# Splitting the W1 load into pieces of 3, 2, 3 and 4 column blocks, with the x tiles moved behind them

## The chip, the cores and the metric

The kernel runs on one core of one Trainium2 chip. The metric is the device time of one execution in microseconds (us), as a median over repeated executions. Kernels are compared only within the same rounds. The span of a profile is about 1.7 us shorter than the device time of the same run.

## The reference

A transformer block with two branches in parallel on the same normalised input. The change touches only the layer norm and the first matrix product of the second branch.

```python
xn = _layernorm(x)                        # x: 2048 x 640, bf16
return x + _A_ref(xn, wqkv, wo) + _B_ref(xn, w1, b1, w2, b2)

def _B_ref(x, w1, b1, w2, b2):            # w1: 640 x 1536
    h = _gelu(jnp.einsum("bsd,df->bsf", x, w1) + b1)
    return jnp.einsum("bsf,fd->bsd", h, w2) + b2
# _A_ref: linear attention with 32 heads; not touched by the change
```

## The kernel before

The 2048 tokens are 16 tiles of 128. A tile is loaded (`dma_x`), VectorE takes its statistics in two halves (`ln_half`) and aggregates them (`ln_aggr`), GpSimd makes rstd (one over the standard deviation), and VectorE normalises (`ln_norm`). The normalised tile must then be transposed. Tiles 0 to 2 are transposed by TensorE, and the result is copied out of PSUM, the memory that TensorE writes to. Tiles 3 to 15 are transposed by a DMA. Below, x3 is the load of tile 3, xn(2) the normalised tile 2 and xnT(2) its transpose, and so on. `W1` has 12 column blocks of 128 (`JT` = 12), loaded in four pieces. A unit `(t0, n, jb)` of the first matrix product (the first GEMM below) multiplies block `jb` with `n` tiles from tile `t0` on: five matmuls of n x 128 columns, then a Gelu on ScalarE. `plan` is the order in which TensorE (PE in the profile) runs the units. "T1" and "T2" in it are the places of the transposes of tiles 1 and 2.

```python
W1P = [(i * F // 4, (i + 1) * F // 4) for i in range(4)]      # four pieces of 3 blocks
...
dma_x(0, 1); dma_x(1, 1)                                      # one queue, in this order
dma_w1(0); dma_w1(1)
dma_x(2, 1); dma_x(3, 1)
dma_w1(2); dma_x(4, 2); dma_w1(3); dma_x(6, 2)
...
def copy2(t, b0, b1):      # xnT(t) out of PSUM: 3 parts by ScalarE, 2 by VectorE  (cut)
def h_unit(t0, n, jb):     # reads the W1 piece of jb and xnT of its tiles          (cut)
...
plan = h_list(0, 1, 0, 3) + ["T1"] + h_list(0, 1, 3, 6) + h_list(1, 1, 0, 6)
plan += h_list(0, 2, 6, 7) + ["T2"] + h_list(0, 2, 7, 9) + h_list(2, 1, 0, 9) + h_list(0, 3, 9, JT)
plan += h_list(3, 1, 0, 3) + h_list(4, 1, 0, 3) + h_list(3, 2, 3, JT) + h_list(5, 3, 0, JT)
plan += h_list(8, 2, 0, 3) + h_list(10, 2, 0, 3) + h_list(8, 4, 3, JT) + h_list(12, 4, 0, JT)
for u in plan:
    if u == "T1":
        transp2(1, b, b + 1); copy2(1, b, b + 1)
        ln_stats(2); ln_half(3, 0); ln_half(3, 1); ln_norm(2); ln_aggr(3); ln_half(4, 0)
    elif u == "T2":
        b = transp(2); xnT_copy(2, b)
        ln_norm(3); xnT_dma(3); ln_half(4, 1); ln_aggr(4); ln_rest()
    else:
        h_unit(*u)
```

Each engine runs its instructions in the order in which they stand. So an instruction that waits for a late tile holds up whatever stands behind it on its engine, even work on another tile.

## Time and profile before

| kernel before | |
|---|---|
| device time, 3 runs | 207.26 us median (207.16 to 207.52) |
| profiled run: time, span | 207.4 us, 205.6 us |
| PE busy | 202.2 us, 98% of the span |
| first GEMM: its first matmul, its end (where the chain passes to the next stage) | 6.63 us, 59.75 us |
| T2 transposes begin | 10.99 us |

From the page of the kernel before: its engines' busy time, and the engines of the chain of waits that ended last.

```profile
PE 202.2 (98%) x1539; PEld 135.2 (66%) x1539; DVE 109.6 (53%) x227; ACT 71.4 (35%) x133; POOL 35.1 (17%) x85
...
PE 96%; DVE 1%; DMA 1%; issue 0%; ACT 0%; DVEq 0%
```

PE is nearly always busy and the chain runs through it, so a change elsewhere shows only where it makes PE wait or stop waiting. The chain in order of time shows where that could be. Its columns are start, length and what; L380 is the first GEMM, L318 and L361 are the transposes T1 and T2, L488 is the stage behind the first GEMM.

```profile
6.63 1.00 PE ps L380 x15
7.63 0.28 PE ps L318 x5
7.91 0.01 issue
7.92 3.23 PE ps L380 x50
11.15 0.28 PE ps L361 x5
11.43 48.32 PE ps L380 x340
59.75 21.73 PE ps L488 x160
```

No visible gap. But the ends of matmuls are modelled in this view, and short waits hide in their tails. The weight loads (PEld) show them better. From their timeline (start, busy time, engine, line, operation, count, then in brackets the idle time before it and what ended it):

```profile
6.60 0.85 PEld L380 LDWEIGHTS ps<-xnT,W 128*128 128x128 bf16 x15 [0.23 <-DMA W<-in_B_w_dram]
7.41 0.32 PEld L318 LDWEIGHTS ps<-ident,xn_tm 128*128 128x128 bf16 x5
7.92 2.95 PEld L380 LDWEIGHTS ps<-xnT,W 128*128 128x128 bf16 x50 [0.19 <-DMA W<-in_B_w_dram]
10.88 0.37 PEld L361 LDWEIGHTS ps<-ident,xn_tm 128*128 128x128 bf16 x5
```

The third line is the one hole that the change can close: PE stands 0.19 us for the second W1 piece. The fourth line has no bracket: the transposes of tile 2 come when PE gets to them, and xn(2) is already there. How much earlier is read on VectorE (DVE):

```profile
7.95 0.29 DVE L327 COPY xnT<-ps 128x256 bf16<-128x256 bf16 x1 [0.80 <-PE ps L318]
8.36 0.89 DVE L331 BATCH_NORM_STATS2 stats<-xPK 128x6 f32<-128x320 bf16 x2
9.35 0.21 DVE L339 BATCH_NORM_AGGREGATE aggr<-stats 128x2 f32<-128x12 f32 x1
9.47 0.83 DVE L331 BATCH_NORM_STATS2 stats<-xPK 128x6 f32<-128x320 bf16 x2
10.32 0.45 DVE L353 TENSOR_SCALAR xn_tm<-xPK,aggr,rstd 128x640 bf16<-128x640 bf16 x1
```

These are, in order, the copy for tile 1, the statistics of tile 2, both halves of tile 3's statistics, and the normalisation of tile 2. It ends at 10.77 us (10.32 + 0.45), 0.11 us before PE's weight loads for it begin (10.88).

### The profile page before, as it was taken

The page shows a single profiled execution, that of the slowest core. Times are in us where ns is not written, and L with a number is a line of the kernel's source. Part 1 is how long each engine was busy: PE and PEld are TensorE (multiplying, and loading weights), DVE is VectorE, ACT ScalarE, POOL GpSimd, SP SyncE. Part 2 cuts the span into 40 slices and gives each one's busy share as a digit, 9 for nine tenths or more (in the row PEclk, how much of TensorE's full clock was granted, in tenths as well). Part 3 has the DMA queues.
Part 4 walks back from the last instruction along what each step waited for, and adds up shares of the span by engine and source line. Part 5 has one row for each costly group of instructions (what it writes and reads, how often), then busy time and mean ns, then how long its engine had stood idle before and what let it go on. Part 6 is the DMA issues. An engine that isn't in the chain of part 4 may idle for free.

```text
span 205.6 us, 3863 instructions
## 1 busy us (share of the span) xinstructions
PE 202.2 (98%) x1539; PEld 135.2 (66%) x1539; DVE 109.6 (53%) x227; ACT 71.4 (35%) x133; POOL 35.1 (17%) x85
## 2 busy tenths in 40 slices
PE   8999999999999999999999999999999999999995
PEld 3898767544457777777746445677777777777774
DVE  3784388100007888999358888734764322523322
ACT  2787777666676455111153554300000000000000
POOL 3342156800000001999000200000000000000000
PEclk9999999999999999999999999999999999999999
DMA  5967846699920000000000000968611100100111
GB/s 153 351 169 122 204 127 123 81 360 327 368 90 0 0 0 3 0 0 3 0 0 3 2 0 19 364 182 171 152 64 63 35 32 32 37 32 32 35 37 59
DMA packets 24842, 19.69 MB, mean 96 GB/s; under 512 B 9976, under 2 KB 24824, under 8 KB 24824
## 3 DMA queue, kind: packets, MB, share of 16 engines
q1 hardware_dynamic: 23072, 17.86, 29.5%
q10 hardware_dynamic: 1752, 1.58, 4.1%
q8 instruction: 12, 0.20, 0.4%
q14 instruction: 6, 0.05, 0.1%
HBM read 13.11 MB, written 2.62 MB: 77 GB/s over the span
## 4 chain that ended last, share of the span: by engine, by line
PE 96%; DVE 1%; DMA 1%; issue 0%; ACT 0%; DVEq 0%
PE ps L671 36%; PE ps L380 26%; PE ps L513 11%; PE ps L488 11%; PE ps L554 10%; DMA xPK<-in_A_x_dram 1%; DVE stats L331 1%; PE ps L608 1%; PE ps L564 1%; PE ps L618 1%; PE ps L318 0%; DVE xn_tm L353 0%; DVE W L722 0%; PE ps L361 0%; PE ps L537 0%
## 5 line engine op out<-in xcount | busy, mean ns | idle before, releaser
L671 PE MATMUL ps<-W,HG 128*128 128x320 bf16 (+2 forms) x396 | 54.8, 295 | 0.0
L380 PE MATMUL ps<-xnT,W 128*128 128x128 bf16 (+3 forms) x405 | 52.7, 292 | 0.1
L671 PEld LDWEIGHTS ps<-W,HG 128*128 128x128 bf16 x396 | 38.1, 98 | 14.5 <-ACT Msb L590 0.2
L380 PEld LDWEIGHTS ps<-xnT,W 128*128 128x128 bf16 x405 | 33.8, 98 | 18.4 <-DMA W<-in_B_w_dram 0.4
L384 ACT ACTIVATE HG<-ps,b1c 128x128 bf16<-128x128 f32 (+3 forms) x81 | 39.1, 515 | 14.4 <-PE ps L380 13.3
L682 DVE TENSOR_TENSOR W<-ps,xnT 128x640 bf16<-128x640 f32 x15 | 12.4, 825 | 35.8 <-PE ps L671 34.6
L476 ACT ACTIVATE ek<-ps 128x512 bf16<-128x512 f32 (+1 forms) x36 | 23.2, 645 | 20.4 <-PE ps L554 10.7
L477 DVE TENSOR_SCALAR ek<-ek 128x512 bf16<-128x512 bf16 (+1 forms) x36 | 11.0, 305 | 32.4 <-ACT ek L476 31.2
L671 PE MATMUL ps<-Msb,PQ 128*128 128x320 bf16 (+2 forms) x165 | 24.2, 295 | 0.0
L554 PE MATMUL ps<-xnT,Wqkv 128*128 128x512 bf16 x100 | 21.9, 379 | 0.0
L513 PE MATMUL ps<-xPK,xn_tm 128*128 128x320 bf16 x160 | 21.9, 299 | 0.0
L488 PE MATMUL ps<-Wqkv,xnT 128*128 128x320 bf16 x160 | 21.9, 299 | 0.0
L671 PEld LDWEIGHTS ps<-Msb,PQ 128*128 128x128 bf16 x165 | 15.9, 98 | 5.9
L488 PEld LDWEIGHTS ps<-Wqkv,xnT 128*128 128x128 bf16 x160 | 15.7, 98 | 6.2
L513 PEld LDWEIGHTS ps<-xPK,xn_tm 128*128 128x128 bf16 x160 | 15.7, 98 | 6.1
L507 POOL COPY Wqkv<-Wqkv 128x128 bf16<-128x128 bf16 x25 | 15.1, 603 | 22.9 <-PE ps L488 21.4
L331 DVE BATCH_NORM_STATS2 stats<-xPK 128x6 f32<-128x320 bf16 x32 | 14.0, 477 | 9.3 <-DMA xPK<-in_A_x_dram 9.2
L554 PEld LDWEIGHTS ps<-xnT,Wqkv 128*128 128x128 bf16 x100 | 9.7, 98 | 11.4
L479 DVE SCALAR_TENSOR_TENSOR PQ<-ps,ek 128x512 bf16<-128x512 f32 x20 | 13.8, 692 | 2.1
L479 DVE SCALAR_TENSOR_TENSOR xPK<-ps,ek 128x640 bf16<-128x640 f32 x16 | 13.2, 825 | 1.7
L525 DVE TENSOR_TENSOR Msb<-Msb,xPK 128x640 f32<-128x640 f32 x14 | 11.6, 825 | 0.5
L341 POOL TENSOR_TENSOR rstd<-aggr,mhalf 128x1 f32<-128x1 f32 x16 | 9.9, 620 | 8.9 <-DVE aggr L339 8.9
(57 smaller groups left out, 77.4 us busy)
## 6 DMA issues: line engine op xcount, KB each, us to landing
xnT<-in_A_x_dram SPq DMA_DIRECT2D x4, 640.0 KB, 6.8
Wqkv<-in_A_wqkv_dram SPq DMA_DIRECT2D x3, 800.0 KB, 6.8
out_dram<-W SPq DMA_DIRECT2D x15, 160.0 KB, 1.8
W<-in_B_w_dram SPq DMA_DIRECT2D x4, 480.0 KB, 6.1
W<-in_B_w_dram SPq DMA_DIRECT2D x1, 1920.0 KB, 13.0
xn_tm<-rden ACTq DMA_DIRECT2D x12, 128.0 KB, 3.4
xPK<-in_A_x_dram SPq DMA_DIRECT2D x4, 320.0 KB, 5.5
Wo<-in_A_wo_dram SPq DMA_DIRECT2D x8, 160.0 KB, 8.4
```

The lines of the kernel that those rows point to most:

```text
L331: Pl.ins(v, lambda e: e.bn_stats(stats[:, s, 6 * h:6 * h + 6], x_in[:, t, h * HW:(h + 1) * HW]), reads=r_x[t], writes=[r_stats[s][h]])
L380: Pl.ins(pe, [(lambda e, k=k: e.matmul(bank(b, 0, w), W1[:, k, jb * P:(jb + 1) * P], xnT[:, k, tok], start=(k == 0), stop=(k == DT - 1))) ...
L384: Pl.ins(s_, lambda e: e.activation(HG[:, jb, tok], bank(b, 0, w), ACT.Gelu_apprx_tanh, bias=b1c[:, jb:jb + 1]), reads=[B_[b], r_b1c], wri ...
L476: Pl.ins(s_, lambda e: e.activation(e2, src, ACT.Exp), reads=br, writes=[r_ek[s]])
L479: Pl.ins(v, lambda e: e.scalar_tensor_tensor(out=d2, in0=src, scalar=0.0, in1=e2, op0=ALU.max, op1=ALU.add), reads=br + [r_ek[s]], writes= ...
L488: fns.append(lambda e, k=k, h=h, b=b, t=t: e.matmul(bank(b + h, 0, HW), xnT[:, k, t * P:(t + 1) * P], Wqkv[:, k, D + h * HW:D + (h + 1) * ...
L507: Pl.ins(g, lambda e, k=k, i=i: e.tensor_copy(plain(Wqkv[:, k, D:2 * D], i), parts(Wqkv[:, k, 0:D], i)), reads=[r_Wq], writes=[r_Wk, r_WqP])
L513: Pl.ins(pe, [(lambda e, t=t, h=h, b=b, f=f, i=i: e.matmul(bank(b + h, 0, HW), xn_tm[:, t, f * P:(f + 1) * P], PK[:, t, h * HW:(h + 1) * H ...
L525: Pl.ins(v, lambda e, t=t: e.tensor_tensor(out=zsum, in0=zsum, in1=PK[:, t, :], op=ALU.add), reads=[r_PK[t], r_zsum], writes=[r_zsum])
L554: Pl.ins(pe, [(lambda e, k=k, j=j, b=b: e.matmul(bank(b), Wqkv[:, k, D + j * P:D + (j + 1) * P], xnT[:, k, cc], start=(k == 0), stop=(k == ...
L671: Pl.ins(pe, [(lambda e, i=i, x=x, bb=bb: e.matmul(bank(bb, 0, x[1] - x[0]), seq[i][0], seq[i][1][:, x[0]:x[1]], start=(i == 0), stop=(i = ...
L682: Pl.ins(v, lambda e: e.tensor_tensor(out=halves(out_sb[:, s, :]), in0=pair(b), in1=halves(x_res[:, t, :]), op=ALU.add), reads=B_[b:b + 2] ...
```

## The change

The intent is to let the loads follow what TensorE needs first. The second W1 piece becomes smaller, so that it lands sooner. x3 moves behind the third piece, x4 and x5 behind the fourth, where x6 and x7 already stood. The plan follows the new pieces, which saves two units (81 to 79, ten matmuls), and VectorE's order is adapted to x3 and x4 coming later.

```diff
-        W1P = [(i * F // 4, (i + 1) * F // 4) for i in range(4)]
+        W1J = [0, JT // 4, JT * 5 // 12, JT * 8 // 12, JT]
+        W1P = [(lo * P, hi * P) for lo, hi in zip(W1J, W1J[1:])]
@@
         dma_w1(0)
         dma_w1(1)
         dma_x(2, 1)
+        dma_w1(2)
         dma_x(3, 1)
-        dma_w1(2)
+        dma_w1(3)
         dma_x(4, 2)
-        dma_w1(3)
         dma_x(6, 2)
@@
-        plan = h_list(0, 1, 0, 3) + ["T1"] + h_list(0, 1, 3, 6) + h_list(1, 1, 0, 6)
-        plan += h_list(0, 2, 6, 7) + ["T2"] + h_list(0, 2, 7, 9) + h_list(2, 1, 0, 9) + h_list(0, 3, 9, JT)
+        j1, j2, j3 = W1J[1:4]                                  # 3, 5, 8
+        plan = h_list(0, 1, 0, j1) + ["T1"] + h_list(0, 1, j1, j2) + h_list(1, 1, 0, j2)
+        plan += h_list(0, 2, j2, j2 + 1) + ["T2"] + h_list(0, 2, j2 + 1, j3) + h_list(2, 1, 0, j3) + h_list(0, 3, j3, JT)
@@ at T1
                 ln_stats(2)
                 ln_half(3, 0)
+                ln_norm(2)
                 ln_half(3, 1)
-                ln_norm(2)
                 ln_aggr(3)
-                ln_half(4, 0)
@@ at T2
-                ln_half(4, 1)
-                ln_aggr(4)
+                ln_stats(4)
                 ln_rest()
```

## The prediction

> **What bounds the kernel now.** The page gives PE 202.2 of the 205.6 us span (98%), and the chain of waits is 96% PE; from 6.63 us to the end it is an unbroken row of matmuls. The change can win only (a) a hole in PE before 12 us, or (b) matmul time, and can lose only by opening a hole.
>
> (a) In the view of waits, the first GEMM's weight loads idle 0.4 us behind W1 DMAs, in two pieces. The first is at the start, untouched. The second lies before 7.92 us: tile 1's transposes are through at about 7.74, and the second W1 piece lands at 7.9 (issued 2.2, 5.7 us to landing). Worth 0.18 us.
>
> (b) The plan shrinks from 81 to 79 units (405 to 395 matmuls) with equal columns. In the timeline, 45 matmuls of 128 columns and 5 of 256 between 7.92 and 10.99 make about 56 ns for 128 columns, where the Trainium skill ("TensorE: Matmul & The Clock Gate", "Wait — 56ns, not 53.3ns?") has N/2.4 GHz plus about 2.5 ns; the trace agrees. Ten fewer are worth 0.03 us. So at most 0.2 us of 207 can be won.
>
> **What moves.** In 6 to 12 us the queue runs at 316 to 372 GB/s (windows), about the 358 GB/s HBM limit per core of the skill's "DMA: Bandwidth & Descriptors", "Specifications"; so order alone matters, and landings follow cumulative bytes. Measured landings: W1 first 6.4, second 7.9, x2 8.36, x3 8.7, third 10.3, x4-5 11.2, fourth 12.65, x6-7 13.4. Estimates for the new order: second 7.45, x2 7.9, third 9.4, x3 9.8, fourth 11.7, x4-5 12.5, x6-7 13.4. x3 comes a microsecond later.
>
> **The new start (estimates).**
> 1. Tile 1's transposes end 7.74; piece two is there: 0.18 us gained.
> 2. Only two units (10 matmuls, 0.56 us) now stand before tile 1's own units, which need ScalarE's copy of xnT(1); that ended at 8.41 and doesn't move. PE waits from 8.30 to about 8.47: the gain goes back.
> 3. 25 matmuls of 128 and 5 of 256 columns: PE reaches T2 at about 10.4; piece three is there.
> 4. T2 transposes xn(2). VectorE's tile 1 copy lasts to 8.24, so stats(2) starts only 0.1 earlier (8.26), rstd(2) is ready about 10.1. In front of norm(2) stands the first half of stats(3), now waiting for x3: 9.8 to 10.25. Norm(2) ends about 10.7; the transposes begin 10.65 to 10.85. Before, T2 came after 7 blocks on two tiles (10.99 us), which hid this chain; now after 6. PE waits 0.25 to 0.45 us.
> 5. Then PE has 10 x 107, 40 x 56 and 20 x 160 ns to tile 3's first unit: about 17.5 against 17.28 before. Tiles 4 to 7 are normalised some 0.5 us later, but tile 4's transpose lands near 17.7, needed at 18.4; later margins are about 1 us. No further hole.
>
> **Prediction.** +0.25 us: 207.5 us, 207.05 to 207.95 in 8 of 10. Faster by over 2%: 1%; within 2%: 98%; slower by over 2%: 1%.
>
> **What would show it.** No weight-load wait on a W1 DMA near 7.9; new PE waits on ScalarE's xnT copy near 8.3, and of 0.2 to 0.45 us at T2 on VectorE's xn_tm; stats(3) waiting for x3; 395 matmuls on the first GEMM's line; PE unbroken from 12 us on.
>
> **What would make it wrong.** x3 landing near 9.4 [...] leaves T2 waiting only 0.2 us: about 207.3. After 10.2 costs more. If tile 4 or the fourth piece came a microsecond late, a hole would open after 15 us.

## The result

The changed kernel took 207.80 us in the median (207.54 to 208.00, 6 runs) against 207.33 us for the kernel before (207.16 to 207.52, 6 runs). The ratio is 1.0021, with a 95% interval of 1.0008 to 1.0034. The change is thus about 0.44 us slower: within 2%, but clear of the noise.

| profiled run | before | after |
|---|---|---|
| device time, us | 207.40 | 207.81 |
| PE busy, us | 202.2 | 202.9 |
| matmuls of the first GEMM | 405 | 395 |
| first matmul of the first GEMM, us | 6.63 | 6.92 |
| T2 transposes begin, us | 10.99 | 10.90 |
| from there to the end of the first GEMM, us | 48.76 | 49.30 |
| end of the first GEMM, us | 59.75 | 60.20 |

From the page of the changed kernel:

```profile
PE 202.9 (98%) x1529; PEld 135.4 (66%) x1529; DVE 109.6 (53%) x227; ACT 71.1 (34%) x131; POOL 35.1 (17%) x85
...
PE 98%; DVE 0%; issue 0%
```

PE has ten matmuls fewer and yet 0.7 us more busy time. Some 0.5 us of that are filler matmuls that ran longer at the start (below); and the waits of this section hide in modelled tails, so that the page counts them as busy. This is why a busy share of 98% proves nothing here. The chain of the changed kernel in order of time (L381 is the first GEMM, L319 and L362 are the transposes T1 and T2):

```profile
6.97 0.95 PE ps L381 x15
7.92 0.28 PE ps L319 x5
8.20 0.56 PE ps L381 x10
8.76 0.00 issue
8.76 2.11 PE ps L381 x30
10.87 0.02 issue
10.90 0.45 PE ps L362 x5
11.35 48.85 PE ps L381 x340
60.20 21.73 PE ps L488 x160
```

Between T2's start and the end of the first GEMM there are now 49.30 us instead of 48.76. T2 started 0.09 us earlier, so the first GEMM ends 0.45 us later. What follows is equally long in both: subtracting the end of the first GEMM from the device time leaves 147.65 and 147.61 us. The weight loads of the changed kernel show why T2 is not earlier:

```profile
7.98 0.60 PEld L381 LDWEIGHTS ps<-xnT,W 128*128 128x128 bf16 x10
8.75 1.84 PEld L381 LDWEIGHTS ps<-xnT,W 128*128 128x128 bf16 x30 [0.17 <-ACT xnT L327]
10.89 0.28 PEld L362 LDWEIGHTS ps<-ident,xn_tm 128*128 128x128 bf16 x5 [0.30 <-DVE xn_tm L354]
```

The wait for the second piece is gone (first line, no bracket). There are two new waits: 0.17 us for ScalarE's copy of tile 1 and 0.30 us at T2 for VectorE's normalisation. And VectorE:

```profile
8.24 0.29 DVE L328 COPY xnT<-ps 128x256 bf16<-128x256 bf16 x1 [1.06 <-PE ps L319]
8.44 0.88 DVE L332 BATCH_NORM_STATS2 stats<-xPK 128x6 f32<-128x320 bf16 x2
9.42 0.21 DVE L340 BATCH_NORM_AGGREGATE aggr<-stats 128x2 f32<-128x12 f32 x1
9.82 0.49 DVE L332 BATCH_NORM_STATS2 stats<-xPK 128x6 f32<-128x320 bf16 x1 [0.19 <-DMA xPK<-in_A_x_dram]
10.39 0.45 DVE L354 TENSOR_SCALAR xn_tm<-xPK,aggr,rstd 128x640 bf16<-128x640 bf16 x1
```

The normalisation of tile 2 starts at 10.39 us against 10.32 before. It did not get earlier, while PE now has one block less to do in front of it.

One more difference needs care. The first GEMM of this profile starts 0.29 us later (6.92 against 6.63), although both kernels have the same instructions on PE up to there. The 16 filler matmuls that keep PE running until the first tile is there took 5.07 us against 4.57.

### The profile page after: what moved, and what is told of

It is laid out like the page before. It is cut to its first block, busy times and chain, and to the rows that moved or that the text cites. A ratio compares the mean times of both kernels' runs of the same rounds, so it can differ in the third digit from the quotient of the medians.

```text
span 206.1 us, 3840 instructions
## 1 busy us (share of the span) xinstructions
PE 202.9 (98%) x1529; PEld 135.4 (66%) x1529; DVE 109.6 (53%) x227; ACT 71.1 (34%) x131; POOL 35.1 (17%) x85
## 4 chain that ended last, share of the span: by engine, by line
PE 98%; DVE 0%; issue 0%
PE ps L671 36%; PE ps L381 25%; PE ps L488 11%; PE ps L513 11%; PE ps L554 10%; PE ps L303 3%; PE ps L608 1%; PE ps L564 1%; PE ps L618 1%; PE ps L319 0%; PE ps L362 0%; DVE W L722 0%; PE ps L537 0%; PE ps L309 0%
## 5 line engine op out<-in xcount | busy, mean ns | idle before, releaser
L381 PE MATMUL ps<-xnT,W 128*128 128x128 bf16 (+3 forms) x395 | 52.8, 295 | 0.0
L381 PEld LDWEIGHTS ps<-xnT,W 128*128 128x128 bf16 x395 | 33.6, 98 | 18.6 <-ACT xnT L327 0.2
L525 DVE TENSOR_TENSOR Msb<-Msb,xPK 128x640 f32<-128x640 f32 x14 | 11.6, 826 | 0.5
```

What stands on the lines that cost most here:

```text
L381: Pl.ins(pe, [(lambda e, k=k: e.matmul(bank(b, 0, w), W1[:, k, jb * P:(jb + 1) * P], xnT[:, k, tok], start=(k == 0), stop=(k == DT - 1))) ...
L525: Pl.ins(v, lambda e, t=t: e.tensor_tensor(out=zsum, in0=zsum, in1=PK[:, t, :], op=ALU.add), reads=[r_PK[t], r_zsum], writes=[r_zsum])
```

## The experiments

The theory: T2 asks for xn(2) one block on two tiles (ten matmuls of 56 ns, 0.56 us) sooner than before, but xn(2) comes no sooner; PE waits, and the block that used to cover this wait is done later, with nothing left to cover. Rival A: x3's later landing costs the time. Rival B: the later start of the first GEMM costs it.

In all fourteen profiles, device time minus the end of the first GEMM lies between 147.60 and 147.65 us. So each profile's end of the first GEMM gives that run's time, and the tables below quote it. All outputs were correct.

### The changed kernel again

`e4_after_again` has no edit.

> The changed kernel once more, for the spread of its start. Theory: ratio 1.0015 to 1.0025 again, T2 wait about 0.3 us again, with the first GEMM starting somewhere between 6.6 and 6.95 us by the filler matmuls' clock. If its start is early (6.6) and T2 is still at 10.8 to 10.9, the start isn't the cause (against rival B).

Measured: 207.81 us median (207.60 to 207.89), ratio 1.0019 (1.0005 to 1.0032). This time the first GEMM started at 6.67 us, as early as in the kernel before, and its end was 60.19. From the weight loads and VectorE's timeline of this run:

```profile
8.50 1.84 PEld L381 LDWEIGHTS ps<-xnT,W 128*128 128x128 bf16 x30 [0.18 <-ACT xnT L327]
10.89 0.28 PEld L362 LDWEIGHTS ps<-ident,xn_tm 128*128 128x128 bf16 x5 [0.55 <-DVE xn_tm L354]
...
9.99 0.49 DVE L332 BATCH_NORM_STATS2 stats<-xPK 128x6 f32<-128x320 bf16 x1 [0.61 <-DMA xPK<-in_A_x_dram]
10.40 0.43 DVE L354 TENSOR_SCALAR xn_tm<-xPK,aggr,rstd 128x640 bf16<-128x640 bf16 x1
```

The start moved by 0.25 us, the end by 0.01, and the wait at T2 grew from 0.30 to 0.55 us. With the start of the kernel before (6.67 against 6.63) the whole loss is still there (an end of 60.19 against 59.75), so rival B falls. That the end did not move at all is partly chance: in this run x3 landed at 9.97 instead of 9.80, and it is what holds the normalisation. Where the start and x3 both came earlier, T2 came earlier too (10.54 in `e12_after_x8_early` below).

### T2 one unit later

```diff
-plan += h_list(0, 2, j2, j2 + 1) + ["T2"] + h_list(0, 2, j2 + 1, j3) + h_list(2, 1, 0, j3) + h_list(0, 3, j3, JT)
+plan += h_list(0, 2, j2, j2 + 2) + ["T2"] + h_list(0, 2, j2 + 2, j3 + 1) + h_list(2, 1, 0, j3 + 1) + h_list(0, 3, j3 + 1, JT)
```

> The changed kernel with the transposes of tile 2 (T2) put one two-tile unit later (after units 5 and 6 of tiles 0 and 1) and tile 2's own units run to 9 as before. Theory (T2 comes 0.56 us too soon for xn(2), which is ready near 10.85 us whatever PE does): the PE wait at T2 shrinks from 0.30 to under 0.1 us, and the time is that of the kernel before, ratio 0.9990 to 1.0005 (207.1 to 207.45 if before is 207.33). Rival A (x3 landing late costs the time by itself): no change, ratio about 1.002. Rival B (a later start of the first GEMM, 6.92 against 6.63 us, costs the time, through filler matmuls at a low clock): ratio anywhere from 1.000 to 1.002, following the start in the profile and not T2.

Measured: 207.47 us (207.35 to 207.62), ratio 1.0005 (0.9993 to 1.0018). Start 6.67, T2 at 11.01 without a wait, end of the first GEMM 59.77:

```profile
8.51 2.66 PE ps L381 x35
11.18 0.28 PE ps L362 x5
11.45 48.32 PE ps L381 x340
59.77 21.73 PE ps L488 x160
```

The remainder after T2 is 48.76 us again. The loads, the piece sizes and VectorE's order are those of the changed kernel; only the plan differs (tile 2 also gets its block 8 as a unit of its own, so there are 80 units). This one line takes back the loss as far as the noise tells. The intervals of the two ratios overlap, but in the same rounds its five runs took 207.35 to 207.62 us and those of the changed kernel 207.60 to 207.89. So rival A in its strong form falls too: VectorE waits for x3 here as well (until 9.56), and it harms nothing once PE doesn't ask so soon. x3 came early in this profile, but even with x3 at 9.97 the weight loads of T2 could begin at 10.89 (`e4_after_again`), and here PE came to them at 10.90.

### The normalisation of tile 2 first, and x3 early

`e2_norm_first` takes x3 out of the way on VectorE, `e3_x3_early` in the queue.

```diff
@@ e2_norm_first
                 ln_stats(2)
+                ln_norm(2)
                 ln_half(3, 0)
-                ln_norm(2)
                 ln_half(3, 1)
@@ e3_x3_early
         dma_x(2, 1)
+        dma_x(3, 1)
         dma_w1(2)
-        dma_x(3, 1)
         dma_w1(3)
```

> The changed kernel with the normalisation of tile 2 put before the first half of tile 3's statistics on VectorE, so that it no longer stands behind x3. Theory: it is then held by rstd(2), ready 10.1 to 10.3 us, so T2 begins 10.65 to 10.85 and 0.05 to 0.2 us of the loss comes back: ratio to before 1.0008 to 1.0018. Rival A (x3 is the whole cause): the loss is gone, ratio 1.000. Rival B: no change beyond the start's shift, ratio 1.001 to 1.003.

> The changed kernel with x3 back beside x2, before the third W1 piece; sizes and plan stay changed. x3 should land near 8.3 us. Theory: T2 held by rstd(2) as in the run that normalises tile 2 first, starts 10.65 to 10.85, ratio 1.0008 to 1.0018; third W1 piece lands near 9.8 and is not waited for. Rival A: ratio 1.000. Rival B: as the changed kernel.

Measured: 207.72 us, ratio 1.0017 (1.0005 to 1.0030) and 207.81 us, ratio 1.0015 (1.0003 to 1.0028). Both intervals exclude the 1.000 that rival A expected here. T2 began at 10.84 and 10.89, the first GEMM ended at 60.24 and 60.19. Both profiles had a late start (6.87 and 6.92). What held the normalisation is now another thing. First the run with the normalisation first, then the one with x3 early:

```profile
8.39 0.88 DVE L332 BATCH_NORM_STATS2 stats<-xPK 128x6 f32<-128x320 bf16 x2
9.37 0.21 DVE L340 BATCH_NORM_AGGREGATE aggr<-stats 128x2 f32<-128x12 f32 x1
10.34 0.45 DVE L354 TENSOR_SCALAR xn_tm<-xPK,aggr,rstd 128x640 bf16<-128x640 bf16 x1 [0.76 <-POOL rstd L342]
```

```profile
10.39 0.45 DVE L354 TENSOR_SCALAR xn_tm<-xPK,aggr,rstd 128x640 bf16<-128x640 bf16 x1 [0.40 <-POOL rstd L342]
```

With x3 out of the way, VectorE waits for rstd(2). From the start of tile 2's statistics to its normalisation it is 1.95 us (8.39 to 10.34, 8.44 to 10.39), and the statistics stand behind VectorE's copy for tile 1, which waits for T1. So two gates stand side by side: x3, and T1 plus about 2.6 us (7.71 to 10.34, 7.75 to 10.39). In the changed kernel's second profile, with an early start, x3 is the later gate: 10.40, where the other by this sum would have been near 10.14. In its first profile, with a late start, the other is the later one: 10.39, where x3 would have let the normalisation start near 10.23 (its statistics at 9.82, plus the 0.41 us that lie between the two in the second profile). So removing x3 alone wins nothing when the start is late, as it was in both of these profiles, and within their intervals both kernels stay where the changed kernel is. With an early start it may win something: of the five runs with x3 early, three took 207.81 us and two 207.47 and 207.53, but the faster two weren't profiled.

### The order of loads alone, and with VectorE's order

Both keep four pieces of 3 and the plan of before. `e5_order_only` has the three moved load lines of the change; `e7_order_dve` has these and the moved `ln_norm(2)` and `ln_half(4, ·)`.

> The kernel before with nothing but the changed order of loads (x2 behind the second W1 piece, third piece, x3, fourth piece, x4-5); its four pieces of 3, its plan and its VectorE order stay. x3 should land near 10.2 us and x4-5 near 12.5 us. In the old VectorE order the normalisation of tile 2 stands behind both halves of tile 3's statistics, and the copy of xnT(2) behind the first half of tile 4's. Theory: T2 begins near 11.6 (a hole of 0.6 us), the units of tile 2 wait once more, for the copy, until about 13.5; about 1.2 us slower, ratio 1.004 to 1.007. Rival A in its strong form (any late x3 costs what the change cost): 1.002. Rival B: 1.000.

> The kernel before with the changed order of loads and the changed VectorE order, but with four pieces of 3 and the plan of before (T2 after 7 blocks). Theory: the VectorE order takes back most of the loss of the load order alone; x3 near 10.2, normalisation of tile 2 from 10.7, T2 near 11.2 against 10.99 before: 0.2 us slower, ratio 1.0003 to 1.0015. If the changed VectorE order were itself the cost, this would be at 1.002 or more.

Measured: the order alone 208.58 us (208.29 to 209.29), ratio 1.0059 (1.0046 to 1.0073); with VectorE's order 207.93 us (207.75 to 208.10), ratio 1.0026 (1.0013 to 1.0039). From PE's timeline of the order alone:

```profile
11.50 0.45 PE L361 MATMUL ps<-ident,xn_tm 128*128 128x128 bf16 x5 [0.31 <-DVE xn_tm L353]
11.79 1.25 PE L380 MATMUL ps<-xnT,W 128*128 128x256 bf16 x10
13.55 0.62 PE L380 MATMUL ps<-xnT,W 128*128 128x128 bf16 x8 [0.50 <-DVE xnT L369]
```

Two holes, both foretold: T2 waits for the normalisation behind both halves of tile 3's statistics, and the units of tile 2 wait for a copy that stands on VectorE behind the statistics of tile 4, whose load landed at 12.58. The VectorE order of the change cures the second and shortens the first (T2 at 11.36, end of the first GEMM 60.13). So it is a necessary companion to the new order of loads. The second expectation was too low: x3 landed at 10.43, not 10.2, and the first GEMM of the profiled run ended 0.38 us later than in the kernel before. That run (207.75) was the fastest of its five; why the others were another 0.2 us slower wasn't profiled.

### T1 one unit earlier, and all three repairs

`e8_t1_early` is the run with the normalisation first, plus T1 after two units. `e9_t1_early_t2_later` adds the later T2 of `e1_t2_later`.

```diff
-plan = h_list(0, 1, 0, j1) + ["T1"] + h_list(0, 1, j1, j2) + h_list(1, 1, 0, j2)
+plan = h_list(0, 1, 0, j1 - 1) + ["T1"] + h_list(0, 1, j1 - 1, j2) + h_list(1, 1, 0, j2)
```

> The changed kernel with the normalisation of tile 2 first on VectorE and the transposes of tile 1 (T1) one unit earlier (after 2 units of tile 0 instead of 3). Theory: ScalarE's copy of xnT(1) ends near 8.2 and three units cover it, so PE no longer waits for it; the whole VectorE chain of tile 2 moves 0.28 us earlier to rstd(2) near 9.8 to 10.1, T2 at 10.35 to 10.65, PE there at 10.25 to 10.5. Ratio 0.9993 to 1.0006; the PE wait at T2 0.1 to 0.2 us. If T2's lateness came from x3 alone, the earlier T1 would bring nothing over the run with the normalisation first (1.0017).

> All three repairs: T1 one unit earlier, normalisation of tile 2 first, T2 one two-tile unit later, tile 2's own units to 9. Theory: no PE wait of 0.05 us or more from the first GEMM's start on; all that is left of the 0.2 us that the pieces of 3, 2, 3, 4 can win: ratio 0.9987 to 0.9998. If it is at 1.000 or above, there is a cost of the piece sizes that I haven't named.

Measured: `e8_t1_early` 207.69 us (207.61 to 208.00), ratio 1.0017 (1.0005 to 1.0029), a miss. The mechanism held in its profile: with a late start (6.92) T2 came at 10.61, 0.23 and 0.28 us earlier than in `e2_norm_first` and `e3_x3_early`, and PE no longer waited for ScalarE's copy. But 0.1 us was given back: with both halves of tile 3's statistics between the normalisation and the copy of xnT(2), the units of tile 2 waited 0.2 us on weight loads for that copy, as in `e2_norm_first`. The end of the first GEMM was 60.01, and this run (207.61) was again the fastest of its five. I don't know what the others lost.

`e9_t1_early_t2_later`: 207.42 us (207.24 to 207.82), ratio 1.0001 (0.9989 to 1.0013), also above what was expected. T2 began at 10.85 without a wait, and with the usual 48.76 us behind it the end would have been 59.61. It was 60.20, and the missing 0.59 us are two holes. The first, of about 0.12 us, is at 11.6 us: PE comes to block 8, the first of the fourth W1 piece, before that piece has landed (11.74), and its weight loads wait 0.23 us. It is the second wait of this line of PEld's waits (us in total, times, longest):

```profile
PEld ps L381 <- DMA W<-in_B_w_dram: 0.5, 2, 0.2
```

This is a cost of the piece sizes that I hadn't named: with T1 early and T2 late, block 8 comes too soon for a fourth piece of four blocks. At 35.15 PE's weight loads run dry, 24.30 us after T2; the kernel before has that work behind it 24.18 us after T2 (35.17), which makes the 0.12. The second hole, the remaining 0.46 us or so, follows there. PE's and PEld's timeline:

```profile
35.70 1.33 PEld L381 LDWEIGHTS ps<-xnT,W 128*128 128x128 bf16 x13 [0.55 <-issue]
35.74 1.47 PE L381 MATMUL ps<-xnT,W 128*128 128x256 bf16 x12 [0.30 <-issue]
```

The profile names no releaser, but these are the units of tiles 10 and 11, and tile 11's DMA transpose, issued at 33.08 and 2.6 us on its way, landed at 35.65. Loading of tiles 8 to 15 is issued behind the transposes of tiles 3 to 7, at 21.74 us in this run, at 20.7 to 20.8 in the two profiles of the changed kernel, and at 20.0 in both profiles of the kernel before. The change has made this chain 0.7 us later. The other 1.0 us is this run's own: the transpose of tile 6 took 4.2 us to land instead of 2.6, and the issue of tile 7's lasted 2.3 us instead of 1.3. The same shows in the profiles of `e5_order_only` and `e7_order_dve` (loads at 22.52 and 22.00) and not in that of `e8_t1_early` (20.82); what decides it stays open. In the kernel before, tile 11's transpose landed at 33.86 and its weight loads began at 35.18. In the two profiles of the changed kernel it landed at 34.53 and 34.95, for weight loads at 35.63 and 35.62, so there it was still in time. The profiled run was the slowest of its five (207.82); the other four were 207.24 to 207.42.

### Loading tiles 8 to 11 sooner

To close that hole I issued x8-9 behind the transpose of tile 5 and x10-11 behind that of tile 6, in the kernel with all repairs, in the kernel before, and in the changed kernel.

```diff
             out(5)
+            dma_x(8, 2)
             ln_stats(7)
             out(6)
+            dma_x(10, 2)
             out(7)
-            dma_x(8, 2)
-            dma_x(10, 2)
             dma_x(12, 4)
```

> The kernel with all three repairs (T1 early, normalisation of tile 2 first, T2 later), and the loads of x8-9 and x10-11 issued behind the transposes of tiles 5 and 6 instead of behind that of tile 7. In the profile of the kernel without this last step PE stood 0.3 us before the units of tiles 10 and 11, whose transposes had come late. Theory: PE is unbroken from the first GEMM's start to its end; that end is at 59.5 to 59.7 us (59.75 before), and with the rest of the program at a constant 147.6 us the time is 207.1 to 207.3: ratio 0.9985 to 0.9997. If it is 1.000 or above, the hole before tile 11 wasn't what ate the gain.

> The kernel before with nothing but the earlier loads of x8-9 and x10-11. There tile 11's transpose landed 1.3 us before it was needed. Theory: nothing to win, ratio 0.9993 to 1.0007. If this is faster by itself, the gain of the run with all repairs isn't the gain of the piece sizes.

> The changed kernel with nothing but the earlier loads of x8-9 and x10-11. Theory: its loss arises at T2 and not at tiles 8 to 11, so it stays: T2 at 10.8 to 10.95, end of the first GEMM at 60.1 to 60.25, ratio 1.0012 to 1.0025. If it comes back to 1.000, the loss was in the later tiles.

Measured: 209.13 us, ratio 1.0082 (1.0067 to 1.0096); 208.70 us, ratio 1.0058 (1.0042 to 1.0073); 209.83 us (208.93 to 211.86), ratio 1.0119 (1.0082 to 1.0155). All three expectations failed, and the profiles show one reason in all three. PE's timeline of the kernel before with this edit, and then of the changed kernel with it:

```profile
25.17 2.11 PE L380 MATMUL ps<-xnT,W 128*128 128x384 bf16 x12 [1.00 <-DMA xnT<-xn_tm]
```

```profile
25.46 1.79 PE L381 MATMUL ps<-xnT,W 128*128 128x384 bf16 x10 [1.30 <-DMA xnT<-xn_tm]
```

With a load of 320 KB in front of each, the transposes of tiles 6 and 7 took 5.1 and 5.2 us from issue to landing in the first of these runs, against 2.6 and 3.8 in the kernel before without the edit. In no profile without this edit did either take more than 4.3 us. They missed the units of tiles 5 to 7. In the run with all repairs, PE's weight loads also waited 0.46 us for the fourth W1 piece, until 11.82. Why the other five runs of the changed kernel with this edit took 0.15 to 2.9 us more than the profiled one (208.93) wasn't profiled. The repair opened a larger hole than it was to close. Since the edit brings this loss by itself to the kernel before, the totals decide nothing about tiles 8 to 11. One thing can still be read: in the changed kernel with this edit the first GEMM started at 6.51 us, x3 landed at 9.6, and T2 came at 10.54, the earliest seen. x3 was the later gate there: VectorE normalised at 10.05, 0.41 us after x3's statistics began, where T1 (7.34) plus 2.63 us would have given 9.97.

### The kernel before against itself

> The kernel before against itself, for the spread: ratio 0.999 to 1.001, and one more profile of its start. If its first GEMM starts late (near 6.9) this time, its end should be late by no more than about 0.1 us (the hole before the second piece takes up 0.18 of the 0.27).

Measured: 207.33 us, ratio 0.9997 (0.9981 to 1.0012); start 6.71, T2 10.96, end of the first GEMM 59.72. The late start that I wanted came instead in the kernel before with the early loads of tiles 8 to 11, which is the same up to there: it started at 6.92, and T2 came at 11.09, 0.10 us later than with the start at 6.63. The hole before the second W1 piece took up the rest of the 0.29 us.

## Why the prediction was right

The time (207.80) lies in the range (207.05 to 207.95), and the sign and the place were right. The range holds the 207.33 us of the kernel before as well, so the time alone would not tell the forecast mechanism from no change at all; the waits that were foretold do. The size was off: 0.44 us where 0.25 was forecast. Point by point:

- **Landings.** The estimates from cumulative bytes held. In the first profile of the changed kernel the second piece landed at 7.36 (7.45 was estimated), x2 at 7.84 (7.9), the third at 9.33 (9.4), x3 at 9.80 (9.8), the fourth at 11.65 (11.7), x4-5 at 12.54 (12.5); in the second profile each came 0.16 to 0.19 us later, x3 at 9.97. Between 7 and 12 us the DMAs of the first profile moved 349 to 362 GB/s in windows of 1 us; the Trainium skill's "DMA: Bandwidth & Descriptors", "Specifications", has a limit of about 358 GB/s of HBM per core. The trace lies at this figure; that the limit is what sets the rate, no run here shows.
- **Steps 1 and 2.** The wait for the second piece vanished, and a wait of 0.17 us for ScalarE's copy took its place (0.17 was estimated). But the two don't enter the sum: PE waits at T2 in both profiles (0.30 and 0.55 us), so that xn(2), and not what PE gained before, sets the time.
- **Step 3.** PE at T2 near 10.4: in the profile with an early start the weight loads begin at 10.89 after 0.55 us of idling, that is from 10.34 on.
- **Step 4, the mis-sized term.** "The transposes begin 10.65 to 10.85" was about 0.1 us too early: 10.84 to 10.90 in the four profiles with T1 and the plan of the change and without the early loads of tiles 8 to 11. The prediction let the normalisation begin at 10.25, behind x3; measured, it began at 10.34 to 10.40. Its steps were right, but their inputs moved. In the first profile T1 came at 7.75 (the kernel before had 7.46, which the prediction took over), and the chain behind T1 was the later gate, not x3. In the second, T1 was early, x3 landed at 9.97, and the normalisation began 0.41 us after the statistics of x3 (9.99). That both ended with T2 at 10.90 and 10.89 is chance. With T1 and x3 as assumed, T2 would have begun near 10.73, inside the forecast (an estimate: statistics of x3 at 9.82, 0.41 us to the normalisation and 0.5 us from there to T2, as in both profiles). By the prediction's own sum, T2 at 10.75 meant +0.28 us; T2 at 10.90 means -0.09 + 0.54 = +0.45 us, which is what was measured.
- **Step 5.** The remainder after T2 was to grow by about 0.5 us (to the first unit of tile 3, 6.51 us of matmuls and 0.3 of transposes against 17.28 - 10.99 = 6.29) and grew by 0.54. No further hole appeared in the profiles of the changed kernel. But tiles 8 and up came 0.7 us later. Tile 11 landed 1.1 and 0.7 us before it was needed in the two profiles of the changed kernel, 1.3 us before it in the kernel before, and the hole in `e9_t1_early_t2_later` shows what another microsecond does.

What stays open: runs of `e7_order_dve` and `e8_t1_early` were slower than the profiled one by up to 0.4 us, those of `e12_after_x8_early` by up to 2.9. For the first two, a late tile 11 as in `e9_t1_early_t2_later` would do it, but that is argued, not shown. Nor was the new plan run with the whole old order of loads. No version beat the kernel before: the best two were at 1.0005 and 1.0001.

## What to carry to other kernels

When a load becomes smaller so that the matrix engine starts sooner, look at the next thing in program order that this engine needs from another engine. If that doesn't come sooner, the work that covered it is merely moved behind the wait, and the loss is about the size of the work moved (0.45 of 0.54 us here). Move the dependent step along with it, as the one-line edit of `plan` did here. A wait with two gates close together does not yield to removing one of them.

## What the Trainium skill lacked or had wrong

- "TensorE: Matmul & The Clock Gate", "Back-to-back issue gap", gives about 81 ns (N = 128) and 131 ns (N = 512) as the sustained spacing in a stream of weight loads and matmuls. Here it was 56 ns at N = 128, and 216 ns at N = 512 (105 matmuls from 37.06 to 59.72 us in the second profile of the kernel before). Both are what its isolated formula N/2.4 + 2.5 says.
- The same page, "What's actually happening", says that the throttle's window is free-running and that the number of slow matmuls at a kernel's start varies. The traces agree with the second: the 16 fillers took 3.97 to 5.07 us in these fourteen profiles, and the first GEMM started between 6.48 and 6.92 us. What it lacks is that the granted clock in the profile doesn't show this: it reads 1.00 from 0.8 us on in the changed kernel, while the fillers of 512 columns came 0.43 us apart, twice the 0.216 us of later ones.
- "DMA: Bandwidth & Descriptors", "DMA Transpose (X-bar)", has no word on the speed of a transpose that stands behind plain loads in one queue (its "Rules for kernel authors" says that "A transpose next to ordinary DMAs needs nothing", which is about correct results). Here such loads took the time to its landing from 2.6 and 3.8 us to 5.1 and 5.2 us (tiles 6 and 7).
- The same page, "Bandwidth", has the rule to batch DMAs to 1 MiB and more for 75% of peak. Loads of 160 to 640 KB, queued one behind the other, moved 349 to 362 GB/s together, so in a full queue loads well under 1 MiB were not slow here. No run varied the size alone.
